# Hash attention on one core: scores and values in groups of three units, hash products and key sums on four column tiles

## The chip, the core and the metric

The kernel runs on one core of a Trainium2 chip. Its engines work side by side and hand work to each other by semaphores: TensorE (PE; its weight loads are shown apart as PEld), VectorE (DVE), ScalarE (ACT), GpSimd (POOL) and SyncE (SP, which issues DMA transfers). Each takes its own instructions in a fixed order. The metric is the time of one execution on the device in microseconds (us), less is better.

## What is computed

Attention with a hash mask, then a layer of 8 experts of which each token takes one (cut from the reference):

```python
B, H, S, D = 4, 8, 768, 64            # batch, heads, sequence, head size
q_bits = (q @ proj) > 0               # proj: D x 6, so 6 bits for each query
k_bits = (k @ proj) > 0
mask = bucket(q_bits)[:, :, :, None] == bucket(k_bits)[:, :, None, :]
scores = where(mask, (q @ k.T) / 8, -1e9)
attn = softmax(scores)                # over the keys
x = (attn @ v) as (B*S, H*D) = 3072 x 512
logits = cosine(x, expert_emb) / tau  # expert = argmax, gate = its softmax
out[t] = gate[t] * (relu(x[t] @ w1[expert]) @ w2[expert])
```

All data is float32; the hash bits are kept as bfloat16.

## The kernel before, in words

Attention works on 16 pairs of heads (`pairs`). `load` fetches q, k and v of a pair by DMA. `prep_features` (once for q, once for k) transposes six 128x128 blocks on TensorE, so that head size lies on the partitions (64 rows for each head of the pair), and copies the result out as `qt` (ScalarE, scaled) and `kt` (VectorE). `prep_bits` multiplies `qt` or `kt` with the projection (`proj2`, 128x128), and one VectorE operation turns the result into bits of bfloat16, `qb` or `kb`.

A pair has 12 units: two halves `s` of 384 queries, six blocks `c` of 128 keys each. `scores(u)` computes for both heads a 128x384 block, keys on the partitions: a float32 product of `kt` and `qt` (line 268) and, added to it in the same banks, a bfloat16 product of the bits (line 271), which pushes down what the mask leaves out. Each head takes 64 rows of TensorE's array, so the two heads are two row tiles (64x128). A float32 matmul is two instructions, and the trace shows four starts for two heads. ScalarE takes the exp (line 274) into a tile `p`; VectorE adds the tiles `p` of a half up into `acc` (lines 278 and 281), whose sum over partitions is the softmax's denominator. `attend(u)` multiplies `p` with v into the bank `av` (line 289): 64 result columns of the array for each head, so two column tiles (128x64). After six units the result is moved out as `o` (line 295).

`finish_half(pr, s)` turns `o` back (three products with `iden`, 144 columns each: the identity and the normalised expert embeddings, line 310), gets the denominators by six products of `acc` with one column of ones (line 312), and VectorE normalises output and logits (lines 314 to 321). After four pairs a batch is complete, and `route` chooses the experts: six squares on ScalarE (line 132), a power on GpSimd (line 150), some small VectorE operations, an exp of `l` on ScalarE.

PSUM has eight banks. A pool of three tiles of two banks each (`banks()`) serves scores, transposes, bits and finish; two single banks serve `av`. The loop writes units in turn: `scores(u)`, `attend(u - 2)`, and from the table `todo` at fixed units one of features, bits, `finish_half` or a load. A scheduler then orders each engine's instructions, chooses the places in the pools, and sets the waits; on TensorE the order stays nearly that of the code.

Behind attention come the counting of tokens for each expert and the expert stretch (31 tiles of 128 tokens, lines 563 and 571), which the change doesn't touch.

Of the kernel before, what the change touches and what calls it, by code (L numbers as in the profile page):

```python
# [25 lines left out]
def kernel(  # L26
# [62 lines left out]

    hrow = const.tile([P, 1], F32, name="hrow")  # L90
    nc.vector.tensor_scalar(out=hrow[:], in0=part[:], scalar1=float(D), scalar2=-float(D), op0=ALU.is_ge, op1=ALU.mult)
    nc.vector.tensor_tensor(out=hrow[:], in0=hrow[:], in1=part[:], op=ALU.add)
# [21 lines left out]
    proj2 = const.tile([P, P], F32, name="proj2")  # L114
    nc.vector.memset(proj2[:], 0.0)
    for h in range(2):
        for r in range(2):
            c0 = h * D + r * NB
            nc.sync.dma_start(proj2[h * D : (h + 1) * D, c0 : c0 + NB], proj[:, :])
# [46 lines left out]
    with ExitStack() as at:  # L166
# [49 lines left out]
        ld, feat, bits, acc, av, xb, lgh = {}, {}, {}, {}, {}, {}, {}  # L216
# [14 lines left out]
        def prep_features(pr, i):  # L231
# [12 lines left out]
            if i == 0:  # L244
                nc.scalar.activation(t[:], ps[:, :, 0:SH], ACT.Copy, scale=DOWN)
            else:
                nc.vector.tensor_copy(out=t[:], in_=ps[:, :, 0:SH])

        def prep_bits(pr, i):
            if pr >= len(pairs):  # L250
                return
            t = augp.tile([P, 2, SH], BF16, name="qb" if i == 0 else "kb", tag="qb" if i == 0 else "kb")
            bits[pr, i] = t
            ps = banks()
            for s in range(2):
                nc.tensor.matmul(ps[:, s, 0:SH], lhsT=proj2[:], rhs=feat[pr, i][:, s, :], start=True, stop=True)
            nc.vector.tensor_scalar(out=t[:], in0=ps[:, :, 0:SH], scalar1=0.0,
                                    scalar2=(qsub if i == 0 else ksub)[:, 0:1], op0=ALU.is_gt, op1=ALU.subtract)


        def scores(u):
            pr, s, c = units[u]
            qt, kt, qb, kb = feat[pr, 0], feat[pr, 1], bits[pr, 0], bits[pr, 1]
# [11 lines left out]
            if c == 1:  # L275
                a = op.tile([P, 2, SH], F32, name="acc", tag="acc")
# [6 lines left out]
        def attend(u):  # L283
# [9 lines left out]
            o = op.tile([P, SH], F32, name="o", tag="o")  # L293
# [4 lines left out]
        def finish_half(pr, s):  # L298
            b, j = pairs[pr]
            if j == 0 and s == 0:  # L300
                xb[b] = xp.tile([P, NC, XW], F32, name="xb", tag="xb")
                lgh[b] = xp.tile([P, NC, E, H], F32, name="lgh", tag="lgh")
            o, a = av.pop((pr, s)), acc.pop((pr, s))
            W = P + 2 * E
            ps = banks()
            t = ps[:, 0, 0 : HC * W].rearrange("p (c w) -> p c w", w=W)
            z = ps[:, 1, 0 : HC * 2].rearrange("p (c h) -> p c h", h=2)
            for c in range(HC):
                cols = slice(c * P, (c + 1) * P)
# [6 lines left out]
            cs = slice(s * HC, (s + 1) * HC)  # L316
            nc.vector.tensor_tensor(
                out=xb[b][:, cs, j * P : (j + 1) * P].rearrange("p c (h d) -> p c h d", d=D),
                in0=t[:, :, 0:P].rearrange("p c (h d) -> p c h d", d=D),
                in1=rz[:].unsqueeze(3).broadcast_to([P, HC, 2, D]), op=ALU.mult)  # L320
            nc.vector.tensor_tensor(
# [14 lines left out]
        for i in range(2):  # L336
            prep_bits(0, i)
# [269 lines left out]
```

## Time and profile before

| | |
|---|---|
| median of 3 runs | 1033.05 us (1031.98 to 1033.67) |
| the profiled execution's own time | 1033.62 us |
| its span, first to last instruction | 1031.9 us |
| TensorE matmul busy | 966.8 us (94%) |
| VectorE / ScalarE / GpSimd busy | 321.0 / 244.9 / 70.0 us |
| mean granted TensorE clock | 0.971 |
| attention, first scores to last finish | about 23 to 511 us |
| experts | about 520 to 1032 us |

Busy time of TensorE is modelled: matmuls overlap in the pipeline, and an instruction's shown duration reaches beyond the start of the next one. So the timeline is read by starts: the distance from one start to the next is what an instruction cost. The page of the profile groups instructions by source line; for each stretch of the span another view adds up busy time by engine and shows the granted clock.

### The profile page before, as it was taken

How to read it: one execution, taken by the hardware profiler on the slowest of the kernel's cores; microseconds unless marked ns; L12 is line 12 of the kernel's file. 1: busy time of each engine (PE TensorE's matmuls, PEld its weight loads, DVE VectorE, ACT ScalarE, POOL GpSimd, SP SyncE). 2: the span in 40 equal slices, each digit the busy share in tenths (PEclk: the TensorE clock that was granted, in tenths of full speed). 3: DMA queues.
4: the chain of work that ended last, by engine and by line, in shares of the span. 5: the costliest groups of instructions: out<-in, count | busy, mean ns of one | idle time of the engine just before them, and what ended most of it. 6: DMA issues, size and time to landing. Idle time of an engine off the chain costs nothing. (4 is left out here: it accounts for less than half of the span.)

```text
span 1031.9 us, 13121 instructions
## 1 busy us (share of the span) xinstructions
PE 966.8 (94%) x5477; PEld 574.0 (56%) x5477; DVE 321.0 (31%) x550; ACT 244.9 (24%) x357; POOL 70.0 (7%) x81
## 2 busy tenths in 40 slices
PE   4999999999999999999736999999999999999996
PEld 2444444444444444444335667766766776677674
DVE  3545546554555456455430000100110010011000
ACT  3443444343544335333300000000000000000000
POOL 1000000000000000000001101110110111011000
PEclk8999999999999999999956999999999999999999
DMA  8111013111121112000018988888898888888860
GB/s 184 31 47 46 17 46 107 32 47 47 31 93 47 31 47 77 1 1 1 1 63 313 353 320 310 311 313 316 314 311 317 312 314 312 320 307 314 304 253 1
DMA packets 109121, 170.57 MB, mean 165 GB/s; under 512 B 53302, under 2 KB 57398, under 8 KB 108545
## 3 DMA queue, kind: packets, MB, share of 16 engines
q1 hardware_dynamic: 104064, 155.23, 45.3%
q0 software_dynamic: 4992, 14.44, 3.5%
q8 instruction: 45, 0.74, 0.3%
q14 instruction: 20, 0.16, 0.0%
HBM read 157.06 MB, written 14.43 MB: 166 GB/s over the span
## 5 line engine op out<-in xcount | busy, mean ns | idle before, releaser
L563 PEld LDWEIGHTS ps_h<-xgt,w1t 128*128 128x128 f32 x1984 | 230.5, 193 | 32.4 <-ACT ht L566 18.1
L563 PE MATMUL ps_h<-xgt,w1t 128*128 128x128 f32 x1984 | 236.5, 278 | 10.8 <-ACT ht L566 10.8
L571 PE MATMUL ps_y<-w2t,ht 128*128 128x512 f32 x496 | 218.0, 592 | 0.0
L274 ACT ACTIVATE p<-banks 128x768 f32<-128x768 f32 x192 | 154.0, 808 | 219.6 <-PE banks L271 194.9
L268 PE MATMUL banks<-qt,kt 64*128 64x384 f32 x768 | 177.4, 539 | 0.2 <-ACT p L274 0.2
L289 PE MATMUL av<-p,vt 128*64 128x385 f32 x768 | 166.4, 512 | 0.1
L281 DVE TENSOR_TENSOR acc<-acc,p 128x768 f32<-128x768 f32 x128 | 122.6, 958 | 116.0 <-ACT p L274 114.9
L571 PEld LDWEIGHTS ps_y<-w2t,ht 128*128 128x128 f32 x496 | 91.9, 190 | 103.8 <-issue 103.8
L566 ACT ACTIVATE ht<-ps_h 128x512 f32<-128x512 f32 x62 | 37.0, 597 | 464.2 <-PE ps_h L563 464.2
L573 DVE TENSOR_SCALAR y<-ps_y,xg 128x512 f32<-128x512 f32 x31 | 23.3, 751 | 323.8 <-PE ps_y L571 323.8
L268 PEld LDWEIGHTS banks<-qt,kt 64*128 64x128 f32 x768 | 58.7, 187 | 81.9 <-issue 77.7
L289 PEld LDWEIGHTS av<-p,vt 128*64 128x64 f32 x768 | 38.0, 134 | 91.9 <-issue 89.2
L271 PE MATMUL banks<-qb,kb 64*128 64x384 bf16 x384 | 63.6, 325 | 0.0
L574 POOL DMA_INDIRECT out_dram<-y,src x31 | 31.5, 1015 | 409.4 <-DVE y L573 409.4
L551 DVE COPY xgt<-ps_x 128x512 f32<-128x512 f32 x31 | 21.5, 692 | 110.8 <-PE ps_x L549 100.3
L312 PEld LDWEIGHTS banks<-ones,acc 128*128 128x128 f32 x384 | 51.5, 191 | 0.0
L310 PE MATMUL banks<-iden,o 128*128 128x144 f32 x192 | 47.9, 331 | 0.7 <-DVE o L295 0.7
L312 PE MATMUL banks<-ones,acc 128*128 128x1 f32 x384 | 48.2, 229 | 0.0
L295 DVE TENSOR_SCALAR o<-av 128x384 f32<-128x384 f32 x32 | 19.8, 618 | 68.4 <-PE av L289 68.4
L310 PEld LDWEIGHTS banks<-iden,o 128*128 128x128 f32 x192 | 28.9, 190 | 20.0 <-issue 18.6
L150 POOL TENSOR_TENSOR nrm<-ss,half 128x6 f32<-128x6 f32 x4 | 5.3, 1334 | 488.3 <-ACT sq L132 488.3
L243 PE MATMUL banks<-ident,qk 128*128 128x128 f32 x192 | 29.1, 291 | 8.1 <-DMA qk<-in_q_dram 8.1
(119 smaller groups left out, 417.2 us busy)
## 6 DMA issues: line engine op xcount, KB each, us to landing
w1t<-in_moe_w_dram SPq DMA_DIRECT2D x31, 2048.0 KB, 9.4
w2t<-in_moe_w_dram SPq DMA_DIRECT2D x31, 2048.0 KB, 11.1
xd<-xb SPq DMA_DIRECT2D x4, 1539.0 KB, 5.9
qk<-in_q_dram SPq DMA_DIRECT2D x32, 192.0 KB, 3.6
qk<-in_k_dram SPq DMA_DIRECT2D x32, 192.0 KB, 3.9
vt<-in_v_dram SPq DMA_DIRECT2D x16, 384.0 KB, 3.6
xg<-xd,src POOLq DMA_INDIRECT x31, 7.6
out_dram<-y,src POOLq DMA_INDIRECT x31, 7.7
```

What stands on the lines that cost most here:

```text
L243: nc.tensor.transpose(ps[:, c // HC, (c % HC) * P : (c % HC + 1) * P], qk[:, i, c, :, :], ident[:])
L268: nc.tensor.matmul(ps[:, h, 0:SH], lhsT=kt[rows[h], c // HC, kc], rhs=qt[rows[h], s, :], start=True, stop=False)
L271: nc.tensor.matmul(ps[:, h, 0:SH], lhsT=kb[rows[h], c // HC, kc], rhs=qb[rows[h], s, :], start=False, stop=True)
L274: nc.scalar.activation(p[:, :, 0:SH], ps[:, :, 0:SH], ACT.Exp, scale=ESCALE)
L281: nc.vector.tensor_tensor(out=a[:], in0=a[:], in1=p[:, :, 0:SH], op=ALU.add)
L289: nc.tensor.matmul(ps[h * D : (h + 1) * D, 0 : SH + 1], lhsT=vt[:, h, c, :], rhs=p[:, h, 0 : SH + 1], start=(c == 0), stop=(c == NC - 1))
L310: nc.tensor.matmul(t[:, c, :], lhsT=o[:, cols], rhs=iden[:, j, :], start=True, stop=True)
L312: nc.tensor.matmul(z[:, c, h : h + 1], lhsT=a[:, h, cols], rhs=ones[:, 0:1], start=True, stop=True)
L563: nc.tensor.matmul(ps[:, f, :], lhsT=a[:, d, f * P : (f + 1) * P], rhs=xt[:, d, :], start=(d == 0), stop=(d == ND - 1))
L566: nc.scalar.activation(ht[:, f - 3 : f + 1, :], ps[:, f - 3 : f + 1, :], ACT.Relu)
L571: nc.tensor.matmul(py[:], lhsT=ht[:, f, :], rhs=b[:, f, :], start=(f == 0), stop=(f == NF - 1))
L574: nc.gpsimd.indirect_dma_start(out=out[:, :], out_offset=bass.IndirectOffsetOnAxis(ap=src[:, t : t + 1], axis=0), in_=y[:], in_offset=None ...
```

## The change

Units come in groups of three, four groups to a pair (`g` is 0 to 3): three `scores`, then `attend` for the three units of the group before, then preparation. Group 0 ends with q's features of the next pair and `sums` of the pair before, group 1 with k's features and `finish`, group 2 with `prep_bits` of the next pair and a load; group 3 has nothing more. There are six tiles `p` where there were four.

`prep_bits` handles q and k and both heads in one call: eight matmuls of 32 result columns each (`proj2` is now 128x2x32), on the four column tiles of 32 that the array's columns are divided into, and three VectorE operations where two were (the bits of k lie 32 partitions further down and are moved up). `qb` and `kb` are fixed tiles that GpSimd clears once. `sums` gets the denominators of a whole pair, with ones as 32 stationary columns and `acc` as the moving data, again on four column tiles; ScalarE copies them to `z`, and `finish` transposes `z` by three 128x128 transposes and does both halves of a pair at once. `kt` is copied by ScalarE.

```diff
--- before.py
+++ after.py
...
+    hrow_i = const.tile([P, 1], I32, name="hrow_i")
+    nc.vector.tensor_copy(out=hrow_i[:], in_=part[:])
+    nc.vector.tensor_single_scalar(hrow_i[:], hrow_i[:], 31, op=ALU.bitwise_and)
...
-    proj2 = const.tile([P, P], F32, name="proj2")
+    proj2 = const.tile([P, 2, 32], F32, name="proj2")
...
-        NPT = 4
+        G = 3
+        NPT = 2 * G
...
+        qbs = [ep.tile([P, 2, SH], BF16, name=f"qb{i}") for i in range(2)]
+        kbs = [ep.tile([P, 2, SH], BF16, name=f"kb{i}") for i in range(2)]
+        for t in qbs + kbs:
+            nc.gpsimd.memset(t[:], 0.0)
...
-            if i == 0:
-                nc.scalar.activation(t[:], ps[:, :, 0:SH], ACT.Copy, scale=DOWN)
-            else:
-                nc.vector.tensor_copy(out=t[:], in_=ps[:, :, 0:SH])
-
-        def prep_bits(pr, i):
+            nc.scalar.activation(t[:], ps[:, :, 0:SH], ACT.Copy, scale=1.0 if i else DOWN)
...
+        def prep_bits(pr):
...
             for s in range(2):
-                nc.tensor.matmul(ps[:, s, 0:SH], lhsT=proj2[:], rhs=feat[pr, i][:, s, :], start=True, stop=True)
-            nc.vector.tensor_scalar(out=t[:], in0=ps[:, :, 0:SH], scalar1=0.0,
-                                    scalar2=(qsub if i == 0 else ksub)[:, 0:1], op0=ALU.is_gt, op1=ALU.subtract)
+                for h in range(2):
+                    for i in range(2):
+                        r0 = h * D + i * 32
+                        nc.tensor.matmul(ps[r0 : r0 + 32, s, 0:SH], lhsT=proj2[:, h, :], rhs=feat[pr, i][:, s, :],
+                                         start=True, stop=True)
+            nc.vector.tensor_scalar(out=qb[0:96], in0=ps[0:96, :, 0:SH], scalar1=0.0, scalar2=qsub[0:96, 0:1],
+                                    op0=ALU.is_gt, op1=ALU.subtract)
+            for h in range(2):
+                nc.vector.tensor_scalar(out=kb[h * D : h * D + 32], in0=ps[h * D + 32 : h * D + 64, :, 0:SH], scalar1=0.0,
+                                        scalar2=ksub[h * D + 32 : h * D + 64, 0:1], op0=ALU.is_gt, op1=ALU.subtract)
...
-                a = op.tile([P, 2, SH], F32, name="acc", tag="acc")
+                a = op.tile([P, 2, SH], F32, name="acc", tag="acc", bufs=4)
...
-            o = op.tile([P, SH], F32, name="o", tag="o")
+            o = op.tile([P, SH], F32, name="o", tag="o", bufs=4)
...
-        def finish_half(pr, s):
+        def sums(pr):
+            ps = banks()
+            for s in range(2):
+                for h in range(2):
+                    r0 = 64 * s + 32 * h
+                    nc.tensor.matmul(ps[r0 : r0 + 32, 0, 0:SH], lhsT=ones[:, 0:32], rhs=acc[pr, s][:, h, :],
+                                     start=True, stop=True)
+            z = op.tile([P, SH], F32, name="z", tag="z")
+            zs[pr] = z
+            nc.scalar.copy(out=z[:], in_=ps[:, 0, 0:SH])
...
+        def finish(pr):
...
+            zt = banks()
+            for c in range(HC):
+                nc.tensor.transpose(zt[:, 0, c * P : (c + 1) * P], z[:, c * P : (c + 1) * P], ident[:])
             ps = banks()
...
-                nc.tensor.matmul(t[:, c, :], lhsT=o[:, cols], rhs=iden[:, j, :], start=True, stop=True)
-                for h in range(2):
-                    nc.tensor.matmul(z[:, c, h : h + 1], lhsT=a[:, h, cols], rhs=ones[:, 0:1], start=True, stop=True)
-            rz = small.tile([P, HC, 2], F32, name="rz", tag="rz")
-            nc.vector.tensor_scalar_add(rz[:], z[:], TINY * S)
+            for s in range(2):
+                for c in range(HC):
+                    nc.tensor.matmul(ps[:, s, c * W : (c + 1) * W], lhsT=av[pr, s][:, c * P : (c + 1) * P],
+                                     rhs=iden[:, j, :], start=True, stop=True)
+            rz = small.tile([P, HC, 4], F32, name="rz", tag="rz")
+            nc.vector.tensor_scalar_add(
+                rz[:], zt[:, 0, 0 : HC * P].rearrange("p (c r w) -> p c r w", c=HC, w=32)[:, :, :, 0], TINY * S)
...
-        U, LAG, PU = len(units), 2, 2 * NC
...
-        for u in range(U + LAG + 3):
-            if u < U:
-                scores(u)
-            if 0 <= u - LAG < U:
-                attend(u - LAG)
-            for f, *args in todo.get(u, ()):
-                f(*args)
+        U, PU = len(units), 2 * NC
+        for u0 in range(0, U + PU, G):
+            for u in range(u0, u0 + G):
+                if u < U:
+                    scores(u)
+            for u in range(u0 - G, u0):
+                if 0 <= u < U:
+                    attend(u)
+            pr, g = u0 // PU, u0 % PU // G
+            if g == 0:
+                prep_features(pr + 1, 0)
+                if pr > 0:
+                    sums(pr - 1)
+            elif g == 1:
+                prep_features(pr + 1, 1)
+                if pr > 0:
+                    finish(pr - 1)
+            elif g == 2:
+                prep_bits(pr + 1)
+                load(pr + 3)
```

On TensorE, in the middle of the loop: before, one unit after another, here two units and the step behind them, the transposes of `qk` (in names, `kb` are bits of k as weights, `av` the values' bank).

```order
L268 MATMUL banks<-qt,kt 128x384 x2
L271 LDWEIGHTS kb
L271 MATMUL banks<-qb,kb 128x384
L271 LDWEIGHTS kb
L271 MATMUL banks<-qb,kb 128x384
L289 MATMUL av<-p_158,vt 64x385 x2
L243 MATMUL banks<-ident,qk 128x128 x6
L268 MATMUL banks<-qt,kt 128x384 x2
L271 LDWEIGHTS kb
L271 MATMUL banks<-qb,kb 128x384
```

Now, from the last unit of scores of group 1 to the first of group 2:

```order
L279 MATMUL banks<-qt,kt 128x384 x2
L282 LDWEIGHTS kb_168
L282 MATMUL banks<-qb_166,kb_168 128x384
L282 LDWEIGHTS kb_168
L282 MATMUL banks<-qb_166,kb_168 128x384
L300 MATMUL av<-p_154,vt 64x385 x2
L300 MATMUL av<-p_156,vt 64x385 x2
L300 MATMUL av<-p_158,vt 64x385 x2
L250 MATMUL banks<-ident,qk 128x128 x6
L330 MATMUL banks<-ident,z 128x128 x3
L334 MATMUL banks<-iden,o 128x144 x6
L279 MATMUL banks<-qt,kt 128x384 x2
```

Values of three units stand together, and all of `finish` stands behind the transposes. In the place of banks the third scores of group 3 follow the first scores of that same group; everywhere else scores follow work of an earlier group or step.

On ScalarE, where a batch is complete: before, the squares (`sq`) stand three and three among the exps (`p`).

```order
L274 ACTIVATE p_156<-banks 128x2x384
L132 ACTIVATE sq,ss<-xb 128x512
L274 ACTIVATE p_158<-banks 128x2x384
L132 ACTIVATE sq,ss<-xb 128x512 x2
L274 ACTIVATE p_152<-banks 128x2x384
L274 ACTIVATE p_154<-banks 128x2x384
L274 ACTIVATE p_156<-banks 128x2x384
L274 ACTIVATE p_158<-banks 128x2x384
L245 ACTIVATE qt<-banks 128x768
L274 ACTIVATE p_152<-banks 128x2x384
L132 ACTIVATE sq,ss<-xb 128x512 x3
```

Now:

```order
L285 ACTIVATE p_164<-banks 128x2x384
L251 ACTIVATE kt<-banks 128x768
L133 ACTIVATE sq,ss<-xb 128x512 x6
L285 ACTIVATE p_154<-banks 128x2x384
L285 ACTIVATE p_156<-banks 128x2x384
L156 ACTIVATE l<-l 128x48
L285 ACTIVATE p_158<-banks 128x2x384
L246 ACTIVATE qksq,squares<-qk 128x1536
L285 ACTIVATE p_160<-banks 128x2x384
```

All six squares stand ahead of the exps of group 2 (`p_154` to `p_158`), and the exp of `l` and the squares `qksq` of a later pair stand ahead of group 3's first exp (`p_160`).

On VectorE, around the bits: before, the two evictions stand apart, with adds between them.

```order
L278 TENSOR_TENSOR acc<-p_156,p_158 128x768
L257 TENSOR_SCALAR qb<-banks,qsub 128x768
L281 TENSOR_TENSOR acc<-acc,p_152 128x768
L281 TENSOR_TENSOR acc<-acc,p_154 128x768
L257 TENSOR_SCALAR kb<-banks,ksub 128x768
```

Now:

```order
L292 TENSOR_TENSOR acc<-acc,p_158 128x768
L306 TENSOR_SCALAR o<-av 128x384
L265 TENSOR_SCALAR qb_167<-banks,qsub 96x768
L268 TENSOR_SCALAR kb_169<-banks,ksub 32x768 x2
L292 TENSOR_TENSOR acc<-acc,p_160 128x768
```

Three evictions stand in one piece behind group 2's adds and `o`, ahead of group 3's adds.

## Rows read from the trace of the kernel before

**Rows 1.** Busy time by stretch: engine busy us (instructions), granted clock, DMA share, GB/s.

```profile
core 0: us, PE busy (x) PEld busy (x) DVE busy (x) ACT busy (x) POOL busy (x), PEclk, DMA share, GB/s
23.20:27.10 3.90, 3.90 (x15) 2.11 (x16) 1.41 (x9) 1.91 (x2) 0.00 (x0) 0.50 0.09 32
...
250.00:440.00 190.00, 190.00 (x1091) 87.19 (x1090) 102.75 (x170) 79.34 (x117) 2.65 (x2) 1.00 0.17 49
...
520.00:1032.00 512.00, 471.90 (x2656) 344.40 (x2656) 54.61 (x85) 37.01 (x62) 61.74 (x62) 0.96 0.80 284
```

**Rows 2.** Timeline, TensorE, one unit: start us, shown us, engine, line, tiles, shape, count.

```profile
206.62 0.59 PE L268 MATMUL banks<-qt,kt 64*128 64x384 f32 x2
207.05 0.49 PE L268 MATMUL banks<-qt,kt 64*128 64x384 f32 x2
207.37 0.33 PE L271 MATMUL banks<-qb,kb 64*128 64x384 bf16 x2
207.63 0.54 PE L289 MATMUL av<-p,vt 128*64 128x385 f32 x2
208.00 0.49 PE L289 MATMUL av<-p,vt 128*64 128x385 f32 x2
208.43 0.59 PE L268 MATMUL banks<-qt,kt 64*128 64x384 f32 x2
```

**Rows 3.** Timeline, TensorE, two units of values together at the loop's end.

```profile
505.63 0.82 PE L289 MATMUL av<-p,vt 128*64 128x385 f32 x4
505.95 0.82 PE L289 MATMUL av<-p,vt 128*64 128x385 f32 x4
```

**Rows 4.** Timeline, TensorE, two units of scores together at the loop's start.

```profile
24.62 0.53 PE L271 MATMUL banks<-qb,kb 64*128 64x384 bf16 x2
24.94 0.85 PE L268 MATMUL banks<-qt,kt 64*128 64x384 f32 x2
```

**Rows 5.** Timeline, TensorE, hash products of q and half a finish, each with what follows.

```profile
223.03 1.56 PE L256 MATMUL banks<-qt,proj 128*128 128x384 f32 x4
224.52 0.59 PE L268 MATMUL banks<-qt,kt 64*128 64x384 f32 x2
...
200.85 0.51 PE L310 MATMUL banks<-iden,o 128*128 128x144 f32 x2
...
203.01 0.59 PE L268 MATMUL banks<-qt,kt 64*128 64x384 f32 x2
```

**Rows 6.** Timeline, an exp, what follows one on TensorE, two normalising multiplies.

```profile
207.74 0.81 ACT L274 ACTIVATE p<-banks 128x768 f32<-128x768 f32 x1 [0.99 <-PE banks L271]
...
506.06 0.79 ACT L274 ACTIVATE p<-banks 128x768 f32<-128x768 f32 x1
...
506.91 0.54 PE L289 MATMUL av<-p,vt 128*64 128x385 f32 x2
...
504.78 0.56 DVE L317 TENSOR_TENSOR xb<-banks,rz 128x384 f32<-128x384 f32 x1
...
505.25 0.23 DVE L321 TENSOR_TENSOR lgh<-banks,rz 128x48 f32<-128x48 f32 x1
```

**Rows 7.** Timeline, end of the routing: first square, power on GpSimd, exp of l.

```profile
511.97 0.63 ACT L132 ACTIVATE sq<-xb 128x512 f32<-128x512 f32 x1 [3.89 <-DVE xb L317]
...
513.99 1.32 POOL L150 TENSOR_TENSOR nrm<-ss,half 128x6 f32<-128x6 f32 x1 [109.21 <-ACT sq L132]
...
516.02 0.24 ACT L155 ACTIVATE l<-l 128x48 f32<-128x48 f32 x1 [2.11 <-DVE l L153]
```

**Rows 8.** Groups by line and shape, to 480 us: busy us, mean ns; idle before, releasers.

```profile
L281 DVE TENSOR_TENSOR acc<-acc,p 128x768 f32<-128x768 f32 x119 | 114.0, 958 | 109.0 <-ACT p L274 107.8
...
L239 ACT ACTIVATE qksq<-qk 128x1536 f32<-128x1536 f32 x16 | 23.7, 1482 | 35.0 <-DMA qk<-in_k_dram 35.0
...
L295 DVE TENSOR_SCALAR o<-av 128x384 f32<-128x384 f32 x29 | 17.9, 618 | 63.3 <-PE av L289 63.3
L257 DVE TENSOR_SCALAR qb<-banks,qsub 128x768 bf16<-128x768 f32 x16 | 16.3, 1017 | 4.0 <-PE banks L256 4.0
```

**Rows 9.** Timeline, TensorE, the embedding's transposes ahead of the first scores.

```profile
22.66 0.59 PE L207 MATMUL banks<-ident,en 8*128 8x8 f32 x4 [4.78 <-DVE en L203]
```

More of the change, by code (lines that the diff above doesn't have):

```diff
@@ L88 @@
     tok = iota("tok", [P, B, NC], [[S, B], [1, NC]], base=-N, cm=NC)
+    hrow_i = const.tile([P, 1], I32, name="hrow_i")
+    nc.vector.tensor_copy(out=hrow_i[:], in_=part[:])
+    nc.vector.tensor_single_scalar(hrow_i[:], hrow_i[:], 31, op=ALU.bitwise_and)
     hrow = const.tile([P, 1], F32, name="hrow")
-    nc.vector.tensor_scalar(out=hrow[:], in0=part[:], scalar1=float(D), scalar2=-float(D), op0=ALU.is_ge, op1=ALU.mult)
-    nc.vector.tensor_tensor(out=hrow[:], in0=hrow[:], in1=part[:], op=ALU.add)
+    nc.vector.tensor_copy(out=hrow[:], in_=hrow_i[:])
     ksub = const.tile([P, 1], F32, name="ksub")
@@ L214, in prep_experts @@
                                           in_=ps[h * D : (h + 1) * D, 0, d * E : (d + 1) * E])
-        ld, feat, bits, acc, av, xb, lgh = {}, {}, {}, {}, {}, {}, {}
+        ld, feat, acc, av, zs, xb, lgh = {}, {}, {}, {}, {}, {}, {}
         def load(pr):
@@ new lines, in finish @@
+            rz = small.tile([P, HC, 4], F32, name="rz", tag="rz")
+            nc.vector.tensor_scalar_add(
+                rz[:], zt[:, 0, 0 : HC * P].rearrange("p (c r w) -> p c r w", c=HC, w=32)[:, :, :, 0], TINY * S)
+            nc.vector.reciprocal(out=rz[:], in_=rz[:])
+            for s in range(2):
+                t = ps[:, s, 0 : HC * W].rearrange("p (c w) -> p c w", w=W)
+                r = rz[:, :, 2 * s : 2 * s + 2].unsqueeze(3)
+                cs = slice(s * HC, (s + 1) * HC)
+                nc.vector.tensor_tensor(
+                    out=xb[b][:, cs, j * P : (j + 1) * P].rearrange("p c (h d) -> p c h d", d=D),
+                    in0=t[:, :, 0:P].rearrange("p c (h d) -> p c h d", d=D),
+                    in1=r.broadcast_to([P, HC, 2, D]), op=ALU.mult)
+                nc.vector.tensor_tensor(
+                    out=lgh[b][:, cs, :, 2 * j : 2 * j + 2].rearrange("p c e h -> p c h e"),
+                    in0=t[:, :, P:W].rearrange("p c (h e) -> p c h e", e=E),
+                    in1=r.broadcast_to([P, HC, 2, E]), op=ALU.mult)
+                del av[pr, s]
@@ L332 @@
+            del ld[pr]
+            if j == NP - 1:
+                l = rp.tile([P, NC, E], F32, name="l", tag="l")
+                nc.vector.reduce_sum(out=l[:], in_=lgh.pop(b)[:], axis=AX.X)
+                route(b, xb.pop(b), l, rp)
         for pr in range(3):
@@ L335 @@
             prep_features(0, i)
-        for i in range(2):
-            prep_bits(0, i)
+        prep_bits(0)
         prep_experts()
-        U, LAG, PU = len(units), 2, 2 * NC
-        todo = {}
-        for pr in range(len(pairs)):
-            u = pr * PU
-            todo.setdefault(u + 1, []).append((load, pr + 2) if pr else (load, len(pairs)))
-            for n, (f, i) in enumerate(((prep_features, 0), (prep_features, 1), (prep_bits, 0), (prep_bits, 1))):
-                todo.setdefault(u + 3 + 2 * n, []).append((f, pr + 1, i))
-            for s in range(2):
-                todo.setdefault(u + (s + 1) * NC + LAG + 2, []).append((finish_half, pr, s))
-        for u in range(U + LAG + 3):
-            if u < U:
-                scores(u)
-            if 0 <= u - LAG < U:
-                attend(u - LAG)
-            for f, *args in todo.get(u, ()):
-                f(*args)
+        U, PU = len(units), 2 * NC
[18 more added lines that the diff above has]
+                load(pr + 3)
         most = rp.tile([P, 1], F32, name="most", tag="most")
```

35 lines of the change are left out of this document (7 added, 28 removed).

## Prediction

> **What bounds the kernel now.** I read the table by stretches first. In the attention stretch TensorE is busy in 190.00 of 190 us at a granted clock of 1.00, and the expert stretch behind it lasts 512 us [rows 1]. The change touches attention alone, so the question is what TensorE does there. The timeline of one unit (one key block: scores, then values) answers it, start by start [rows 2]. The score matmuls of float32 start at 206.62 and again at 207.05, the bfloat16 pair at 207.37, the value matmuls at 207.63 and 208.00, the next unit at 208.43: 1.81 us. A "pass" of 384 float32 columns needs 0.32 (207.05 to 207.37), and two tiles of the array (two row tiles in scores, two column tiles in values) share one pass: four starts, two passes. A bfloat16 pass is half, 0.16. Streaming alone is thus 4 x 0.32 + 0.16 = 1.44. What is left, some 0.36, stands where the array changes between 64x128 and 128x64: entering scores 0.43 - 0.32 = 0.11, leaving them 0.26 - 0.16 = 0.10, entering values 0.37 - 0.32 = 0.05, leaving them 0.43 - 0.32 = 0.11. Starts are rounded to 0.01, so I take 0.355 for the four.
>
> Do these gaps vanish between neighbours of one kind? Values: at the loop's end two units of values stand together, and 505.63 to 505.95 is one bare pass [rows 3]. Scores: in the first units, at half clock (0.50 [rows 1]), the bfloat16 pair at 24.62 is followed by the next unit's scores at 24.94 [rows 4]: 0.32 at half clock, 0.16 at full clock, nothing but the stream.
>
> **The change part by part.** (A) Groups of three. Two of three round trips between scores and values go: 2 x 0.355 = 0.71 for each of 64 groups, **-45.4**.
>
> (B) Hash products. Before, one call of four passes takes 223.03 to 224.52 = 1.49 [rows 5], two for each pair of heads, 2.98. Now 8 matmuls of 32 result columns, 16 passes, go to four column tiles. If four run at once, that is 4 x 0.32 + 0.10 to leave + some 0.03 to enter = 1.42. Gain 1.56 on 15 pairs (the first lies under the load of the expert embedding, on which TensorE waits until 22.66 [rows 9]): **-23.4**. Four tiles at once stand in no row; the bounds are 1.42 and, one after another, 16 x 0.323 + 0.13 = 5.30. I take the first, since the nearest rows, the two column tiles of values, lose nothing by sharing.
>
> (C) Finish. Before, half a pair takes 200.85 to 203.01 = 2.16 [rows 5], so 4.32. Now: sums, 8 passes on four tiles, 2 x 0.323 + 0.13 = 0.78 (bounds 0.78 and 2.71); three transposes of z, 128 columns each, on the same scale 128/384 x 0.32 = 0.11, 0.33; six products of 144 columns, 12 instructions of 0.12, 1.46. Together 2.57; gain 1.75 x 16: **-28.0**.
>
> (D) Banks. In group 3 of each pair the third scores get the two banks of the first scores of the same group (the bits have the third place), so they wait for that exp. Counted from the group's start: bfloat16 pair at 0.75, exp 0.37 later (207.37 to 207.74) and 0.81 long [rows 2, 6], TensorE 0.04 to 0.06 behind ScalarE's end (506.06 + 0.79 to 506.91 [rows 6]): 1.98. It would have been ready at 1.72, and pays the weight load anew, 0.11: 0.37 x 16, **+5.9**; zero if the wait is hidden, 0.6 a pair if the exp starts late.
>
> (E) Squares of a finished batch. All six of ScalarE's squares now stand ahead of the three exps of group 2 in 3 of the 16 pairs. Three take 511.97 to 513.99 with what follows, so 0.61 to 0.65 each [rows 7]. Let F be the end of the finish products. The first normalising multiply ends at F + 0.8, six squares at F + 4.5, the first exp at F + 5.3, where the bits want its bank at F + 4.8: 0.5. The second exp ends at F + 6.1; the third stands behind the exp of l, which needs POOL's 1.32 and some 0.7 more [rows 7], so it ends at F + 7.7. Behind it comes qksq, 1.48 [rows 8], then the exp that (D) waits for: the third scores start at F + 10.0, where (D) alone, behind bits 0.5 late, gives F + 6.8 + 2.0. Another 1.2, some 1.8 x 3, **+5.4**; bounds 0 and twice that.
>
> (F) Ends. The last finish now has sums, their copy to z (128x384, between nothing and the 0.81 of a 128x768 exp; I take 0.5 with 0.26 of hand-over, +0.76), and six squares behind it where three were (+1.1); at the start the second group has no values to fill with (+0.5). **+2.4**, bounds 1 and 5.
>
> At nothing: kt's copy moves from VectorE to ScalarE (0.81 as qt's), covered by 1.8 of transposes and finish products ahead of the next use of its banks; each 0.1 that it is late costs 0.1. VectorE's three bit evictions (one 96x768, two 32x768; the nearest row is 128x768, 1.02 [rows 8], bounds a third of it and twice it) replace two. They stand behind the adds and o of group 2 and must end before the next pair's first scores. Counted from group 2's start: two exps end at 1.12 + 1.62, qksq behind them and the third exp at 5.0, its add (0.96) and o (0.62) at 6.6, three evictions at 9.7 [rows 8]; the scores want them at 4.71 + 1.42 + 4.71 + 0.37 = 11.2: cover 1.5. The four multiplies of the finish take 2 x 0.70 [rows 6] and end 1.7 behind F; the third scores of group 2, which take their banks, come at F + 1.8: cover 0.1. Where that is gone, a tenth a pair, 1.6 in all. Queues: the loads on SP are issued three pairs ahead, as late as before against their use; the four memsets on POOL lie ahead of the embedding's power, which waits for a load; if they outlast it, the start moves by the rest.
>
> Sum: -45.4 - 23.4 - 28.0 = -96.8; +5.9 + 5.4 + 2.4 = +13.7; net -83.1. From the profiled execution, 1033.62, that is 950.5; the median of the runs is 0.57 below it, so **950**.
>
> One row and one rule to weigh. Two column tiles share a pass without loss [rows 2]. The Trainium skill, "TensorE: Matmul & The Clock Gate", section "Measured speedup vs the span model", lists three column tiles at 2.38 times one, not three; no run here shows three or four. By the row the sum stays 950; by that figure it is the 958 of a rival below.
>
> **The rivals.** *Four tiles run one after another* (each has its own moving data, which no row shows for four). Bits cost 5.30 - 1.42 = 3.88 more x 15 = 58, sums 1.93 x 16 = 31: 950 + 89 = **1039, slower than before by 6**. For it: nothing in the trace runs four. Against it: two tiles with different moving data start 0.01 apart. It decides where more than 93% (83/89) of the sharing is lost. Chance 0.04.
>
> *Two at a time*, as in the rows: bits 4 more passes (1.29 x 15 = 19.4), sums 2 more (0.65 x 16 = 10.3): **980**. For it: two streams are the most that the trace shows. Chance 0.08.
>
> *Four streams a little slower than one.* At three quarters of full sharing, a pass of 0.41, bits lose 0.34 x 15 and sums 0.17 x 16, 8 in all: **958**. Chance 0.08. The figure of the Trainium skill named above, 2.38 of 3, would give about this.
>
> *Evictions late.* If the short evictions cost twice the row, the bits come 3.05 - 1.5 = 1.55 late on 15 pairs: 23, **973**. For it: the cover is thin and VectorE's queue is in order. Against: VectorE was busy a half of the time. Chance 0.10.
>
> *Grouping saves nothing*, because a gap of 0.1 stands between units of scores at full clock too, where the weight load (0.11) has only a bfloat16 pass of 0.16 to hide in. Two gaps a group, 64 x 0.2 = 13: **963**. Against: the start rows at half clock. Chance 0.05. All other surprises: 0.05.
>
> **How the numbers follow.** My own case, with (D), (E), (F) between their bounds, spans 950 - 12 = 938 to 950 + 12 = 962 and has 0.60, nearly all of it from 941 up. With the cases at 958, 963 and 973, 941 to 975 holds about 0.8; those at 980 and 1039 stay outside. Faster by over 0.2% (2 us, what a measurement of this kernel can tell from no change) 0.94, within 0.01, slower 0.05.
>
> **What would show it.** In the changed profile: a group of three in about 4.7 us, with bare passes between its units; eight hash passes in 1.3 us with four starts within 0.03; TensorE waiting for an exp ahead of the third scores of every fourth group, 0.3 to 0.4; a wait of 1 to 2 in three pairs behind the squares; the expert stretch unchanged at 512. Wrong if the eight hash passes take 2.6 or 5.2, if TensorE waits for kb at the head of a pair, or if starts within a group are 0.1 further apart than the stream.

## The result, and the profile after

The changed kernel takes **949.58 us** (949.05 to 950.25) where the kernel before takes 1033.35 beside it: a ratio of 0.919, 95% interval 0.918 to 0.921. The profiled execution took 949.78, its span is 948.1. One of six executions of a later kernel (groups of three without the waits) took 2304.68 us and is left out of its figures.

| on TensorE, from the span's start | before | after | difference |
|---|---|---|---|
| first scores start | 23.18 | 23.80 | +0.62 |
| from there to the transpose behind the last finish ("most") | 487.42 | 401.63 | -85.79 |
| from there to the first expert matmul | 45.52 | 47.35 | +1.83 |
| from there to the end | 475.79 | 475.29 | -0.50 |

All of the gain lies in attention. The table by stretches after, which answers to [rows 1]:

```profile
250.00:400.00 150.00, 148.58 (x1028) 71.77 (x1026) 96.11 (x141) 78.42 (x110) 1.32 (x1) 1.00 0.13 38
```

TensorE, busy in all of the 190 us of [rows 1], now has small holes: busy 148.58 of 150 us, still at full clock (column 1.00). The expert stretch takes as long as before (475.29 against 475.79). TensorE's timeline shows one group of three, and behind it the hash products of the next pair; it answers to [rows 2] and [rows 5] (start, duration, then instruction and count):

```profile
161.05 0.92 PE L279 MATMUL banks<-qt,kt 64*128 64x384 f32 x4
161.80 0.33 PE L282 MATMUL banks<-qb,kb 64*128 64x384 bf16 x2
161.96 0.81 PE L279 MATMUL banks<-qt,kt 64*128 64x384 f32 x4
162.60 0.33 PE L282 MATMUL banks<-qb,kb 64*128 64x384 bf16 x2
162.77 0.81 PE L279 MATMUL banks<-qt,kt 64*128 64x384 f32 x4
163.41 0.33 PE L282 MATMUL banks<-qb,kb 64*128 64x384 bf16 x2
163.67 2.16 PE L300 MATMUL av<-p,vt 128*64 128x385 f32 x12
165.76 0.51 PE L263 MATMUL banks<-qt,proj 128*32 128x384 f32 x1
165.77 0.51 PE L263 MATMUL banks<-kt,proj 128*32 128x384 f32 x1
165.78 0.51 PE L263 MATMUL banks<-qt,proj 128*32 128x384 f32 x1
165.78 0.51 PE L263 MATMUL banks<-kt,proj 128*32 128x384 f32 x1
166.11 0.49 PE L263 MATMUL banks<-qt,proj 128*32 128x384 f32 x1
...
166.75 0.49 PE L263 MATMUL banks<-qt,proj 128*32 128x384 f32 x1
...
167.19 0.92 PE L279 MATMUL banks<-qt,kt 64*128 64x384 f32 x4
```

The gap of 0.10 behind scores stands once in the group, between 163.41 and 163.67 (0.26 instead of 0.16); from a bfloat16 pair to the next scores it is the bare 0.16. The group takes 161.05 to 165.76, 4.71, where three units took 5.42. The 16 hash instructions start in four lots of four (the first lot from 165.76 to 165.78), 0.32 to 0.35 apart, and the next scores follow at 167.19: 1.43 for what took 2.98. The same timeline at the sums and at the finish:

```profile
177.79 0.85 PE L314 MATMUL banks<-acc,ones 128*32 128x384 f32 x8
178.57 0.92 PE L279 MATMUL banks<-qt,kt 64*128 64x384 f32 x4
...
183.29 0.88 PE L250 MATMUL banks<-ident,qk 128*128 128x128 f32 x6
184.00 0.49 PE L330 MATMUL banks<-ident,z 128*128 128x128 f32 x3
184.33 1.64 PE L334 MATMUL banks<-iden,o 128*128 128x144 f32 x12
185.90 0.92 PE L279 MATMUL banks<-qt,kt 64*128 64x384 f32 x4
```

Sums 0.78, transposes of z 0.33, products with their exit 1.57. Entering the transposes of z from the features costs 0.09 less than entering scores or sums does (183.29 to 184.00 is 0.71, elsewhere the six transposes of the features take 0.80), so the pair pays 2.58 where it paid 4.33.

The holes. First group 3 of an ordinary pair, TensorE and ScalarE:

```profile
66.13 0.92 PE L279 MATMUL banks<-qt,kt 64*128 64x384 f32 x4
...
67.04 0.81 PE L279 MATMUL banks<-qt,kt 64*128 64x384 f32 x4
67.69 0.33 PE L282 MATMUL banks<-qb,kb 64*128 64x384 bf16 x2
68.11 0.92 PE L279 MATMUL banks<-qt,kt 64*128 64x384 f32 x4
...
67.25 1.62 ACT L285 ACTIVATE p<-banks 128x768 f32<-128x768 f32 x2 [0.73 <-PE banks L282]
```

The third scores start 0.42 behind the bfloat16 pair instead of 0.16, 1.98 after the group's start, and last 0.11 longer (their weight load is no longer hidden): 0.37. The first of the two exps, 0.81 long, ends at 68.06, just ahead of them. Then a pair behind which a batch is routed, TensorE and ScalarE:

```profile
142.91 0.33 PE L282 MATMUL banks<-qb,kb 64*128 64x384 bf16 x2
144.32 0.92 PE L279 MATMUL banks<-qt,kt 64*128 64x384 f32 x4 [1.08 <-ACT p L285]
...
138.83 0.19 ACT L133 ACTIVATION_READ_ACCUMULATOR sq<-xb 128x1 f32 x1
138.92 1.48 ACT L285 ACTIVATE p<-banks 128x768 f32<-128x768 f32 x2
141.17 0.24 ACT L156 ACTIVATE l<-l 128x48 f32<-128x48 f32 x1 [0.76 <-DVE l L154]
141.32 0.79 ACT L285 ACTIVATE p<-banks 128x768 f32<-128x768 f32 x1
142.01 1.47 ACT L246 ACTIVATE qksq<-qk 128x1536 f32<-128x1536 f32 x1
143.47 1.50 ACT L285 ACTIVATE p<-banks 128x768 f32<-128x768 f32 x2
```

ScalarE works in its fixed order: the last square ends at 139.0, two exps follow, the third stands behind the exp of l, then comes qksq, and only behind that (143.47) the exp for whose banks TensorE waits until 144.32.

### The profile page after: what moved, and what is told of

Read it like the earlier page. It is cut to its first block, busy times and chain, and to the rows that moved or that the text cites. A ratio compares the mean times of both kernels' runs of the same rounds, so it can differ in the third digit from the quotient of the medians.

```text
span 948.1 us, 12969 instructions
## 1 busy us (share of the span) xinstructions
PE 873.2 (92%) x5397; PEld 538.3 (57%) x5397; DVE 320.5 (34%) x521; ACT 265.1 (28%) x389; POOL 72.8 (8%) x85
## 4 chain that ended last, share of the span: by engine, by line
issue 27%; DMA 24%; PE 1%; DVE 1%; POOL 0%; POOLq 0%; DVEq 0%
DMA out_dram<-y,src 24%; PE slot L546 1%; DVE row L535 0%; POOL xg L569 0%; POOLq L632 0%; DVE col L538 0%; DVE col L540 0%; DVE pos L521 0%; POOLq L604 0%; DVE upto L490 0%; POOLq L569 0%; DVE past L503 0%; DVE pos_e L519 0%; DVE full L494 0%; DVE pos_e L516 0%
## 5 line engine op out<-in xcount | busy, mean ns | idle before, releaser
L279 PE MATMUL banks<-qt,kt 64*128 64x384 f32 x768 | 165.9, 510 | 3.9 <-ACT p L285 2.4
L300 PE MATMUL av<-p,vt 128*64 128x385 f32 x768 | 138.1, 495 | 0.0
L603 DVE TENSOR_SCALAR y<-ps_y,xg 128x512 f32<-128x512 f32 x31 | 23.2, 750 | 323.8 <-PE ps_y L601 323.8
L279 PEld LDWEIGHTS banks<-qt,kt 64*128 64x128 f32 x768 | 64.7, 188 | 69.2 <-issue 37.5
L300 PEld LDWEIGHTS av<-p,vt 128*64 128x64 f32 x768 | 49.5, 136 | 76.5 <-issue 76.5
L289 DVE TENSOR_TENSOR acc<-p,p 128x768 f32<-128x768 f32 x32 | 30.6, 957 | 29.9 <-ACT p L285 29.6
L250 PEld LDWEIGHTS banks<-ident,qk 128*128 128x128 f32 x192 | 21.5, 146 | 26.6 <-issue 25.9
L282 PEld LDWEIGHTS <-kb 64*128 64x128 bf16 x384 | 19.5, 95 | 25.3 <-issue 0.9
L569 POOL DMA_INDIRECT xg<-xd,src x31 | 30.3, 977 | 39.4 <-DVE src L549 30.3
L268 DVE TENSOR_SCALAR kb<-banks,ksub 32x768 bf16<-32x768 f32 x32 | 32.5, 1017 | 0.5
```

Source lines behind the costliest of these rows:

```text
L250: nc.tensor.transpose(ps[:, c // HC, (c % HC) * P : (c % HC + 1) * P], qk[:, i, c, :, :], ident[:])
L268: nc.vector.tensor_scalar(out=kb[h * D : h * D + 32], in0=ps[h * D + 32 : h * D + 64, :, 0:SH], scalar1=0.0, scalar2=ksub[h * D + 32 : h * ...
L279: nc.tensor.matmul(ps[:, h, 0:SH], lhsT=kt[rows[h], c // HC, kc], rhs=qt[rows[h], s, :], start=True, stop=False)
L282: nc.tensor.matmul(ps[:, h, 0:SH], lhsT=kb[rows[h], c // HC, kc], rhs=qb[rows[h], s, :], start=False, stop=True)
L289: nc.vector.tensor_tensor(out=a[:], in0=pts[(u - 1) % NPT][:, :, 0:SH], in1=p[:, :, 0:SH], op=ALU.add)
L300: nc.tensor.matmul(ps[h * D : (h + 1) * D, 0 : SH + 1], lhsT=vt[:, h, c, :], rhs=p[:, h, 0 : SH + 1], start=(c == 0), stop=(c == NC - 1))
```

## The experiments

**Each part alone.** Three kernels, each the kernel before with one part of the change.

Groups only (hash products, sums and finish as before; the calls moved to the groups):

```diff
+        for u0 in range(0, U + PU, G):
+            for u in range(u0, u0 + G):
+                if u < U:
+                    scores(u)
+            for u in range(u0 - G, u0):
+                if 0 <= u < U:
+                    attend(u)
```

> Part A alone: groups of three units; hash products, sums and finish stay as before (two hash calls of four passes, two halves of the finish, kt copied by VectorE). The sum theory: a group of three takes 4.72 where three units took 5.42, 0.70 x 64 = 45 off 1033.3, with up to +10 for waits on exps and evictions that the new order brings (the bits stand in two groups now, so two of the four groups of a pair lack a pair of banks): 988 to 998. Grouping saves nothing between scores: 1001 or more, with starts within a group 0.1 further apart than the stream. The gain of 83.8 not additive (most of it made by the column tiles): 1010 or more.

Measured: 988.09 (987.56 to 988.27) beside 1033.46, **-45.4**. Grouping saves what the gaps said, though the agreement to a tenth is luck: in this order third scores wait for bits in three places (with smaller delays 4.8 by the starts), and about as much is saved where features, hash products and finish, all 128x128, stand side by side (two features in a row take 1.46, apart 2 x 0.80).

Hash products only, in the unit by unit order:

```diff
-                nc.tensor.matmul(ps[:, s, 0:SH], lhsT=proj2[:], rhs=feat[pr, i][:, s, :], start=True, stop=True)
+                for h in range(2):
+                    for i in range(2):
+                        r0 = h * D + i * 32
+                        nc.tensor.matmul(ps[r0 : r0 + 32, s, 0:SH], lhsT=proj2[:, h, :], rhs=feat[pr, i][:, s, :],
+                                         start=True, stop=True)
```

> Part B alone, in the unit by unit order of before: one call of 16 passes on four column tiles in place of two of 4. The sum theory: 2.97 becomes 1.43 on 15 pairs, -23: 1010 (1008 to 1014, if the short evictions delay a pair's first scores here). Four tiles one after another: 5.3 for a call, +35: 1068. Two at a time: 2.7 for a call, -4: 1029. A three-quarter share (the Trainium skill's 2.38 of 3 would give about this): 1.8 for a call, 1015 to 1016.

Measured: 1009.65 (1007.91 to 1010.42), **-23.8**; a call takes 1.43.

Sums and finish only:

```diff
-            for s in range(2):
-                todo.setdefault(u + (s + 1) * NC + LAG + 2, []).append((finish_half, pr, s))
+            todo.setdefault(u + PU + LAG + 2, []).append((sums, pr))
+            todo.setdefault(u + PU + LAG + 4, []).append((finish, pr))
```

> Part C alone, in the unit by unit order of before: sums over keys on four column tiles, z transposed, one finish for a pair. The sum theory: 4.33 becomes 2.58 on 16 pairs, -28, with up to +3 at the end of the last pair: 1005 to 1008. If the sums' four tiles did not share a pass: 0.78 becomes 2.7, +2 for each pair, 1036 to 1039. If the gain of after came from the order of the work rather than from fewer passes: 1020 or more.

Measured: 1008.75 (1008.02 to 1009.09), **-24.7**, just above the range. Sums 0.78 and products 1.57 are as in the changed kernel; z's transposes come straight behind value matmuls here, so they take 0.38 instead of 0.33 and lack the 0.09 that entering from the features saves, some 2 in all; and the way from "most" to the experts is 1.1 longer than before. Together the three give -93.9, the change -83.8: they don't add up by some 10.

**The order of the eight hash matmuls.**

```diff
-            for s in range(2):
-                for h in range(2):
-                    for i in range(2):
+            for h in range(2):
+                for i in range(2):
+                    for s in range(2):
```

> The changed kernel with one thing reordered: the eight hash matmuls are issued tile by tile (both halves of one tile, then of the next) instead of all four tiles, then all four again. Theory that each column tile has its own queue and that a matmul whose tile is free starts past a waiting one: unchanged, 949.6, a call 1.43. Theory that matmuls start strictly in the order of the program: each tile's two instructions of 2 x 2 passes stand in line, so that at most two neighbouring tiles overlap; a call takes 3 to 4.3 instead of 1.43, 24 to 43 more: 974 to 993.

Measured: 948.82 (948.26 to 949.33), no difference. The timeline, TensorE:

```profile
164.54 0.51 PE L263 MATMUL banks<-qt,proj 128*32 128x384 f32 x1
164.56 0.51 PE L263 MATMUL banks<-kt,proj 128*32 128x384 f32 x1
164.57 0.51 PE L263 MATMUL banks<-qt,proj 128*32 128x384 f32 x1
164.58 0.51 PE L263 MATMUL banks<-kt,proj 128*32 128x384 f32 x1
```

The scheduler kept the order: in the program for TensorE both products of one tile stand ahead of the next tile's. Still the first of each tile start within 0.04, ahead of the first tile's second product. So the sharing does not depend on the program alternating the tiles.

**The banks (D).** The hash products leave their banks through ScalarE; VectorE compares the copy.

```diff
+            raw = augp.tile([P, 2, SH], F32, name="raw", tag="raw")
+            nc.scalar.copy(out=raw[:], in_=ps[:, :, 0:SH])
-            nc.vector.tensor_scalar(out=qb[0:96], in0=ps[0:96, :, 0:SH], scalar1=0.0, scalar2=qsub[0:96, 0:1],
+            nc.vector.tensor_scalar(out=qb[0:96], in0=raw[0:96], scalar1=0.0, scalar2=qsub[0:96, 0:1],
```

> The changed kernel, with the hash products first copied out of their two banks by ScalarE (0.81, as qt's copy), and VectorE's three comparisons reading that copy. The bank theory (D): the place that the bits hold comes free after about 1 us instead of after three evictions behind VectorE's queue, so the third scores of group 3 have a free place and the wait of 0.37 goes in 12 or 13 pairs: -4.5 to -6, 944 to 945.5; TensorE starts the third scores 0.16 behind the bfloat16 pair in group 3. Rival, ScalarE's queue is the limit (one more instruction of 0.81 in line with the exps, which the first scores of group 3 wait for): unchanged or up to +5, 949 to 955, with the wait in another place.

Measured: 945.22 (944.23 to 946.01); ratio 0.914 (0.9125 to 0.9156) against 0.919. Attention on TensorE is 5.4 shorter (396.22 from first scores to "most", 401.63 in the changed kernel). Group 3 of an ordinary pair:

```profile
66.58 0.33 PE L284 MATMUL banks<-qb,kb 64*128 64x384 bf16 x2
66.74 0.81 PE L281 MATMUL banks<-qt,kt 64*128 64x384 f32 x4
```

0.16, the bare step. The banks that the bits held were the cause in ordinary pairs: the wait goes in 11 of the 12 that make bits. The first keeps 0.60 from the bfloat16 pair to the third scores, since there the copy stands behind a qksq that waited for its load; in two of the three routed pairs the 1.40 stays too, which belongs to ScalarE's queue.

**The squares (E).** The row norms are left out.

```diff
-        for c in range(NC):
-            sq = rp.tile([P, DM], F32, name="sq", tag="sq")
-            nc.scalar.activation(sq[:], x[:, c, 0:DM], ACT.Square, accum_out=ss[:, c : c + 1])
+        nc.vector.memset(ss[:], 1.0)
```

> The changed kernel without ScalarE's squares of a finished batch (the row norms are left out and set to one, so routing is computed from other norms). Theory E: the waits of about 1.8 that three pairs have behind the squares go (1.6, 1.5 and 0.9 by the trace of the changed kernel, 4.0 together), and the six squares at the end (6 x 0.61 = 3.7) go: 941 to 943. If the waits of those pairs come from elsewhere (POOL's instruction, the exp of l): only the end's 3.7 goes, 945 to 946. If neither lies on the path: 949.6.

Measured: 941.95 (940.69 to 943.19). In the trace attention is 3.2 shorter, the way from "most" to the first expert matmul 3.7. So the squares hold up the three pairs, though not alone: 0.8 of the expected 4.0 stayed. Together with the squares this run takes away what waits for them, GpSimd's power and the lateness of the exp of l; the kernel below with the squares moved out of the line parts the two.

**Group sizes.** One number is changed, `G = 3`, to 4 and to 2.

> The changed kernel with groups of four units, three groups for a pair. Term A for four: 144 round trips saved instead of 128, 16 x 0.35 = 5.6 off 949.6. Against it the banks: a pair has three groups and each now shares its places with features, sums, finish or bits. If only the group that the bits follow waits as now (0.37): 944. If all three groups of a pair wait for the first exp (32 x 0.37 more = 12): 956. Theory: between them, 945 to 956.

Measured: **997.9** (994.98 to 998.69): 42 beyond the range. TensorE at the head of a pair, and its row in the table of waits (total, times, longest):

```profile
159.94 1.56 PE L279 MATMUL banks<-qt,kt 64*128 64x384 f32 x8
162.53 0.49 PE L282 MATMUL banks<-qb,kb 64*128 64x384 bf16 x2 [1.03 <-DVE kb L268]
162.96 0.86 PE L300 MATMUL av<-p,vt 128*64 128x385 f32 x2
```

```profile
PE banks L282 <- DVE kb L268: 22.9, 15, 2.3
```

With three groups to a pair, the hash products stand directly ahead of the scores that use them. The three evictions lie open in each of 15 pairs; besides the wait, the scheduler drew two units' scores and a value matmul forward, which splits the run and brings gaps back. Against the 944 of the easiest case 54 us are lost: 28 of them are waits of TensorE (22.9 here and 5.3 for exps), and about 10 are a lower clock, which the last section shows. I had counted banks and not asked what comes between producing the bits and using them: the rival "evictions late" of the prediction, in a place where it happens.

> The changed kernel with groups of two units, six groups for a pair. Term A for two: 96 round trips saved instead of 128, 32 x 0.35 = 11.3 more than 949.6; term D goes (two scores fit beside the bits): -5. Theory: 953 to 959. If round trips between scores and values were not what the grouping saves: 945 to 950.

Measured: 960.59 (959.35 to 961.83), a little above. By the trace, attention is 10.0 longer than with three: the 11.3 of gaps, less the wait of ordinary pairs, which is gone as said, and some 4 more in the routed pairs, which now wait up to 2.1 for kb (5.1 in three places):

```profile
PE banks L279 <- DVE kb L268: 5.1, 3, 2.1
```

**Four again, with the bits a group earlier.**

```diff
             if g == 0:
                 prep_features(pr + 1, 0)
+                prep_features(pr + 1, 1)
                 if pr > 0:
                     sums(pr - 1)
             elif g == 1:
-                prep_features(pr + 1, 1)
-                if pr > 0:
-                    finish(pr - 1)
-            elif g == 2:
                 prep_bits(pr + 1)
                 load(pr + 3)
+            elif pr > 0:
+                finish(pr - 1)
```

> The groups of four once more, with one thing moved: both features and the sums behind the first group of a pair, the hash products behind the second, the finish behind the third, so that a whole group and the finish lie between the bits and the next pair's first scores. Theory: the 998 of the groups of four came from the bits' evictions having no cover (16 pairs x 3); with cover, what is left is term A for four (-5.6 against 949.6), one switch less a pair for the two features in a row (-1), the third scores behind the bits waiting as now: 942 to 945. Rival, that three pairs of banks are too few for four scores in a row (the fourth scores wait for the first exp in each group): 955 or more, with waits ahead of the fourth scores in all groups.

Measured: 971.2 (968.68 to 975.1). 27 of the 54 is back, so the missing cover was half of it. The time lies in the rival's range, but its sign, waits ahead of the fourth scores in all groups, isn't there; the rest was neither theory. TensorE in the group behind the bits:

```profile
174.89 0.92 PE L279 MATMUL banks<-qt,kt 64*128 64x384 f32 x4 [0.21 <-DVE kb L268]
```

```profile
PE banks L279 <- DVE kb L268: 11.5, 14, 2.1
```

The fourth scores get the banks in which VectorE still reads bits (0.4 to 2.3 us late); in the other groups of ordinary pairs four scores run bare. Another 8.1 in four places are waits for exps, in and behind routed pairs (2.4 in the changed kernel).

**The waits taken away, at three, four and six units.** The bits are copied out as above and the squares spread, two behind each group (three at four units, four at six), columns that are ready a pair earlier first:

```diff
+            if j == NP - 2:
+                x, s1 = xb[b], rp.tile([P, NC], F32, name="s1", tag="s1")
+                first[b] = s1
+                for c in range(NC):
+                    later.append(lambda c=c, x=x, s1=s1: square(x, s1, c, 0, DM - P, rp))
...
+            if pr < len(pairs):
+                some(2)
```

> The changed kernel with groups of three, the bits copied out by ScalarE, and the squares of a batch spread over the groups (two behind each group; the columns that are complete a pair earlier are squared then, so that at the end only the last 128 columns are left). Sum: D and its like go (-5.4, as the copy alone gave), E goes (-3.2, as leaving the squares out gave in attention), the six squares at the end become six short ones (-1.6): 938 to 941. Rival, the squares spread out delay exps everywhere (24 x 0.6 in ScalarE's line): 944 or more.

Measured: **942.16** (941.70 to 942.57), ratio 0.911 (0.910 to 0.9125), against 0.919 for the changed kernel; the best of the runs that compute all. It stays 1.2 short of the range. ScalarE, and TensorE behind it:

```profile
139.13 0.24 ACT L157 ACTIVATE l<-l 128x48 f32<-128x48 f32 x1 [1.70 <-DVE l L155]
139.28 1.48 ACT L254 ACTIVATE qksq<-qk 128x1536 f32<-128x1536 f32 x1
...
141.60 0.92 PE L289 MATMUL banks<-qt,kt 64*128 64x384 f32 x4 [0.90 <-ACT p L295]
```

The squares are out of the way, but the exp of l and qksq still stand in ScalarE's line ahead of an exp, in two pairs. And in the three pairs ahead of the routed ones, where the first columns are squared now, the third scores start 0.43 behind the bfloat16 pair again, 1.1 in all: the copy of the bits comes late there.

> Both: groups of four with the bits a group earlier, the bits copied out, the squares spread. If the terms add: 939.5 for groups of three without these waits, -6.6 for the fourth unit: 932 to 934. If the fourth scores begin to wait for the first exp: 936 or more.

Measured: 950.01 (949.28 to 951.33), 16 above. Two long stops, with what follows them, explain most of it. SyncE's queue, ScalarE, TensorE:

```profile
148.85 0.36 SPq L162 DMA_DIRECT2D xd<-xb  x1
...
153.46 3.71 SPq L241 DMA_DIRECT2D qk<-in_k_dram  x1
...
160.48 1.48 ACT L254 ACTIVATE qksq<-qk 128x1536 f32<-128x1536 f32 x1 [6.42 <-DMA qk<-in_k_dram]
...
162.81 1.65 PE L289 MATMUL banks<-qt,kt 64*128 64x384 f32 x4 [3.63 <-ACT p L295]
...
164.57 1.49 PE L289 MATMUL banks<-qt,kt 64*128 64x384 f32 x4
...
166.17 1.49 PE L289 MATMUL banks<-qt,kt 64*128 64x384 f32 x4
```

The loads of the next q and k now stand in SyncE's queue behind the store of the routed batch (148.85), which waits for VectorE's last routing step (up to 24.4 of SyncE's time); qksq waits for the load, the exp for qksq, TensorE for the exp. These stops are 3.8 and 4.4 long, and the work behind them, at a lower clock (last section), takes some 4 more.

> As the one before with groups of six, two groups for a pair; hash products and sums behind the first, finish and the features of the pair after next behind the second. Another 16 round trips saved, -5.7, if ScalarE keeps up over six units in a row (an exp is 0.81, a unit of scores 0.81): 926 to 929. If ScalarE falls behind (each exp a little later than its bank is wanted): 930 to 945, with waits that grow along the group.

Measured: 945.98 (945.06 to 947.15), just past the rival's range, but not for its reason: in ordinary pairs ScalarE keeps up and six units run bare. The waits stand in the routed pairs and the pairs ahead of them, behind the squares, qksq and the exp of l (0.18, then 0.63 in one group, 1.52 in another), and come to 7.1 over ten places:

```profile
PE banks L289 <- ACT p L295: 7.1, 10, 1.5
```

Attention takes as long as with three (396.1 against 395.5 from first scores to "most"). Of the 11 us of saved gaps these waits, with the exposed weight loads, take back 6 more than with three (10.1 against 3.9 beyond the bare steps), and a wait for an exp ahead of the first hash products another 2.3; what ate the rest stays open.

## Why the prediction was right, step by step

| term | predicted | read in the trace after | by a run |
|---|---|---|---|
| A groups | -45.4 | -45.0 (0.703 x 64) | -45.4 alone |
| B hash products | -23.4 | -23.2 (1.55 x 15) | -23.8 alone |
| C sums, finish | -28.0 | -27.9 (1.74 x 16) | -24.7 alone, with its end |
| D banks | +5.9 | +5.6 | -5.4 in attention when taken away |
| E squares | +5.4 | +4.4 | -3.2 in attention when left out |
| F ends | +2.4 | +2.6 | not tried |
| net | -83.1 | -83.8 (the terms read: -83.5) | -83.8 |

The sum is nearer than its terms: single terms miss by 0.1 to 1.0, in both directions, so a total within 1 us is partly luck.

**A.** The two rare places where neighbours of one kind stood together, two units of values at the loop's end and two of scores at half clock at its start [rows 3, 4], told rightly what the steady loop would do: the gap belongs to the change of kind, not to the unit. The rival that grouping saves nothing fell with 0.16 between units of scores.

**B and C.** The choice between four tiles at once and one after another was the great risk, and the two ends lay 89 us apart. The nearest rows, two tiles sharing without loss [rows 2], carried over to four: 16 instructions in the time of four passes. The rivals at 980 and 1039 fall. The Trainium skill, "TensorE: Matmul & The Clock Gate", section "Measured speedup vs the span model", gives 2.38 of 3 for three tiles; the trace does not agree: at three quarters of the sharing a call would have taken 1.8, and it took 1.43, with the rest of the change and alone. In (C) two errors cancel: the 1.46 for the products left out 0.10 to leave them (1.57 read), and entering from the features costs 0.09 less than the sum had it.

**D.** Predicted 0.37 a pair, read 0.37 in 11 ordinary pairs and 0.52 in the first, where a qksq that waited for its load stands ahead of the exp. It is counted in 15 pairs instead of 16, since behind the last pair no bits are made; in the three routed pairs it is part of a longer wait.

**E.** The chain was right almost to its marks. With F = 134.4, the end of the finish products in the pair shown above (hash products at 139.76): last square F + 4.6 (said 4.5), bits 0.5 late (0.52 read), third scores F + 9.9 (said 10.0). The mis-sized step is the count: three times 1.8 was taken. From hash products to hash products an ordinary pair takes 24.85; the two stretches around each routed batch are together 1.66, 1.62 and 1.07 longer. In the third no qksq stands in the way; half of its 1.07 is that the next pair's first scores wait for the banks that the bits still hold (0.43). And the squares were not its only cause: the exp of l and qksq keep 2 us with the squares out of the way (1.23 and 1.19 from the first bfloat16 pair to the second scores, in the run with groups of three and no squares in line).

**F.** Here the total is near by luck. z's copy showed as expected (sums to transposes 1.45 instead of 0.78, +0.67 against +0.76). The way to the experts grew 1.8, more than the 1.1 of the squares: three more of them at 0.61 are 1.83, so that part was mis-sized. The 0.5 for a second group without values isn't there; its scores run bare. In its place the span before the first scores grew 0.6, the experts shrank 0.5. These two are of the size by which runs differ (first scores start at 23.0 to 23.8 in all traces but that with groups of six, where the next pair's features stand ahead of them).

**Covers.** "At nothing" held: in ordinary pairs the bits were ready 0.9 or more ahead of the product that uses them (cover 1.5 in the sum), and the multiplies of the finish ended 0.3 ahead of the scores that take their banks (cover 0.1). Groups of four showed what the first cover was worth: without it TensorE waits 1.5 a pair, and with the split runs and the clock some 3 are lost. An eviction of 32 partitions takes 1.02, as the row of 128 partitions had it [rows 8]; the page after:

```profile
L268 DVE TENSOR_SCALAR kb<-banks,ksub 32x768 bf16<-32x768 f32 x32 | 32.5, 1017 | 0.5
```

**What the three parts lost together**, 93.9 - 83.8 = 10.1, has the size of D and E (10.0). But it isn't they alone: groups alone have waits and savings of their own, and C alone lacks some 2 (both told above), so part of the sum cancels.

## What to carry to other kernels

Where the engine that sets the time is always busy, price the gaps between kinds of work from its start times, and look for rare places in the same trace where two of a kind stand together: they tell what grouping will save. Then ask of each grouped buffer what must happen between its making and its use: groups of four saved 6 us of gaps and lost 54, half of it because bits were used right where they were made. An in-order queue carries a late load or a routing step into engines that have nothing to do with it, so move a step only after reading what stands in line behind it.

## What the runs showed of the hardware

VectorE's comparison of the bits takes 0.61 from ScalarE's copy (96x768 and 32x768 alike), where it takes about 1.02 from the banks: reading the copy is faster, and 32 partitions take as long as 96.

Stops are dearer than they look. After the 3.63 us for which TensorE stood in groups of four (loads late), units of scores start 1.60 apart instead of 0.81. The table by stretches for that kernel shows why (the last but two column is the granted clock):

```profile
162.80:168.00 5.20, 5.19 (x20) 2.38 (x22) 4.91 (x7) 2.98 (x4) 0.00 (x0) 0.50 0.02 3
```

0.50 is the lower of the two levels, 1.2 GHz; by 172 us the rows are at 1.00 again. Stops of 1.1 us, as in the routed pairs of the changed kernel, leave the next units at their full pace. In the first run with groups of four, where no stop within attention is longer than 2.3, the clock falls too: six times to 0.50, each time shortly behind a stop of 1.75 to 2.12, while other stops of that length, and two of 2.2 and 2.3, leave it at 1.00. Over 400 us of that run the mean is 0.97, where the changed kernel has 1.00; some 10 us are lost by it:

```profile
40.00:440.00 400.00, 372.42 (x2398) 178.92 (x2396) 223.20 (x335) 189.30 (x274) 4.02 (x3) 0.97 0.17 47
```
